# Random-feature attention and a bilinear MLP: norms from bfloat16 halves, q's and k's norms together, a planner with new times and ranks

## The chip, the cores and the metric

One core of a Trainium2 chip runs the whole kernel. The metric is the device time of one execution in microseconds; three executions of the kernel before took 843.41, 843.78 and 844.28 us.

## What is computed

```python
def phi(x):
    proj = np.einsum('bhsd,md->bhsm', x, omega)
    h = proj - np.sum(x * x, axis=-1, keepdims=True) / 2.0
    h = h - np.max(h, axis=-1, keepdims=True)
    return np.exp(h) / np.sqrt(m)
q_p, k_p = phi(q * scale), phi(k * scale)
kv = np.einsum('bhsm,bhsd->bhmd', k_p, v)
z = np.sum(k_p, axis=2)
num = np.einsum('bhsm,bhmd->bhsd', q_p, kv)
den = np.einsum('bhsm,bhm->bhs', q_p, z)[..., None] + 1e-06
x = (num / den).transpose(0, 2, 1, 3).reshape(B * S, H * D)
out = (((x @ w1) * (x @ w2)) @ w3) @ w_out
```

B = 8 batches, H = 8 heads, S = 576 rows, D = 64, m = 128 features; 4608 tokens in all, w1 and w2 are 512x1024, w3 is 1024x1024, w_out is 1024x512. The activations arrive in float32, the weights in float64.

## The kernel before

The 4608 tokens are 36 chunks of 128; a batch is 4.5 chunks. For a chunk of k the kernel projects it on omega (`kpj`), subtracts the maximum (`nm`, L494), adds and takes the exponential (L514, L518) and has the features `ek`; for a batch it sums features times v (`kvp`, L663). A chunk of q goes the same way (`qpj`, `eq`), is turned by two DMA transpositions from SP (`eqT`, L725), and is multiplied with its batch's sums (`nu`, L746). The quotient `xs` is split (`xhl`), turned (`xT`, L804) and enters the gates (`ab`, L981), 256 tokens at a time after the first four chunks. The gates' product goes to `o` (L1022) with the matrix W = w3 w_out, which the kernel forms at the start (`wp`, L932) from weights that it converts from float64 (L828 on ACT, L834 to L854 on DVE).

Precision: where a product is in float16, each operand is two halves, a high part (ACT, or a cast on DVE: L386, L388) and a low part (the difference, on DVE or POOL: L528), and three products are summed. Before a chunk of q or k can be split (`split_raw`, L445: high part L449 on ACT, low part L452 on DVE), it needs a scale, a power of two. `scale` (L430) squares and sums the chunk on ACT into `sums`, `power_of_two` (L348) adds over the partitions by one float32 matmul with ones (L352), and three small steps on DVE (L362 to L366) make the scale of it, a fourth (L440) the factor of the exponential. The first chunks (k below 9, q below 3) are projected in float32 without a scale.

The order of all work is made by `Plan`, in Python, when the kernel is built. Each piece is an operation with an engine (or a choice of engines), a duration in us written beside it, what it reads and writes, and a rank. `order` goes through time: at each moment, each idle engine takes the ready operation of lowest rank whose buffers are free. `LAT` is what passes from an engine's end to the next engine's start, `LANDING` and `US_PER_MB` stand for DMAs. The result is one fixed list per engine, and on the chip each engine works its list off in order. Ranks come from the tables `KRANK`, `QRANK` and `WRANK` for the first chunks and weights, and from `BASE + PERIOD * c` less a lead for the rest. `WEIGHTS_ON_SP` weight blocks are loaded through SP's queue, the others through ACT's; a load has the rank of its block less `FETCH`. `kraw`, `qraw` and `hl` (the split chunks, shared by q and k) have two buffers each, and converted weights pass through three raw buffers.

Of the kernel before, what the change touches and what calls it, by code (L numbers as in the profile page):

```python
# [51 lines left out]
class Plan:  # L52
# [47 lines left out]
    def order(self):  # L100
# [32 lines left out]
        while len(done) < len(self.ops):  # L133
# [5 lines left out]
            for e in ENGINES:  # L139
                if idle[e] > t or not ready[e]:  # L140
                    continue
                for o in ready[e]:
                    took = place(o)
                    if took is not None:
                        break
                else:
# [75 lines left out]
IN_TURN = dict.fromkeys(("kraw", "qraw", "ek", "vraw", "vhl", "kv", "eq", "eqT", "xs", "xhl", "xT", "raw", "mag"), False)  # L222
IN_TURN.update(hl=True, e=True, raw=True, mag=True)


@with_exitstack
def tile_favor_attention_then_bilinear_ffn(
# [65 lines left out]
    def in_pool(pool, shape, dt=F32):  # L293
# [10 lines left out]
        "hl": in_pool(at, (P, 2, NP, P), F16),  # L304
# [43 lines left out]
    def power_of_two(name, cols, keys, n, pre=1.0, add=False, tag="s", n_out=None):  # L348
# [112 lines left out]
    def products(name, c, exact, new=()):  # L461
# [36 lines left out]
    def features(name, c, e, exact, keyed, new=()):  # L498
        pa, pj, nm, factor, key = products(name, c, exact, [e, *new])
        if keyed:  # L500
# [105 lines left out]
    def kv_add(n):  # L606
# [82 lines left out]
    def q_chunk_exact(c):  # L689
# [29 lines left out]
    def q_chunk(c, fast):  # L719
# [3 lines left out]
        for x in range(2):  # L723
# [4 lines left out]
                r=[(t, x)], w=[(u, x)], new=[u] * (x == 0), lat=1.9)  # L728
        eqs[c] = u

    def q_attend(c):
# [68 lines left out]
        if fresh:  # L800
# [165 lines left out]
    def gate(c0, n, u, rank):  # L966
# [4 lines left out]
        for m in range(2):  # L971
            bank = Buf("pm", f"ab_{c0}_{u}_{m}")
            for k in range(nf):
# [92 lines left out]
    om_parts()  # L1066
    for c in range(NCH):
# [5 lines left out]
        else:  # L1073
# [24 lines left out]
    for c in range(NCH):  # L1098
        plan.rank = q_rank(c)
        if c < max(PROJECT_Q, EXACT_Q):  # L1100
            plan.rank -= 20
            load("q", c)
            plan.rank += 20
        else:
# [62 lines left out]
```

## Time and profile before

| | us |
|---|---|
| median of three runs | 843.78 |
| the profiled execution, its own time | 844.44 |
| its span, first to last instruction | 842.3 |
| PE busy | 796.7 (95%) |
| DVE busy | 613.1 (73%) |
| ACT busy | 400.3 (48%) |
| POOL busy | 281.3 (33%) |
| DMA moved | 87.90 MB, mean 104 GB/s |

PE is the matmul engine, PEld its weight loads, which run beside matmuls; SPq and ACTq are the queues from which these engines issue DMAs. A group's busy time counts overlapping instructions once. The granted clock is PE's, as a share of 2.4 GHz; the mean over the run is 0.98. The rows themselves stand below, after the change.

### The profile page before, as it was taken

To read this page: it belongs to the slowest core of one execution; us is meant where nothing else is said; L and a number is where in the kernel's file an instruction comes from. 1 tells how busy PE (TensorE), PEld (TensorE's weight loads), DVE (VectorE), ACT (ScalarE), POOL (GpSimd) and SP (SyncE) were. 2 spreads that over 40 slices of the span, in tenths; PEclk is the share of its full clock that TensorE was granted. 3 is DMA by queue.
4 is the path that set the end of the run, shared out by engine and by line. 5 is a ranking of instruction groups with operands and counts; after the bars stand their busy time and mean duration, and the time that the engine had idled before them with its cause. 6 is when DMAs were issued, how large, how long until landed. Compare 5 with 4: busy or idle time off the path is not lost.

```text
span 842.3 us, 20399 instructions
## 1 busy us (share of the span) xinstructions
PE 796.7 (95%) x8528; PEld 597.6 (71%) x8528; DVE 613.1 (73%) x1177; ACT 400.3 (48%) x697; POOL 281.3 (33%) x287
## 2 busy tenths in 40 slices
PE   3798998899999999999999999899999999999998
PEld 3555546777778777777768677777777777777684
DVE  4889897999969868886769686878696687555200
ACT  3567775665536435543435443745464444322110
POOL 1000001245345253443444453534343533323220
PEclk9598899999999999999999999999999999999999
DMA  9766665114435343534354443433453423322301
GB/s 285 278 234 205 183 181 126 41 41 99 103 62 126 80 98 86 130 90 85 79 82 108 89 76 89 127 77 75 101 127 76 85 61 81 77 52 51 64 26 38
DMA packets 144892, 87.90 MB, mean 104 GB/s; under 512 B 119712, under 2 KB 119840, under 8 KB 144800
## 3 DMA queue, kind: packets, MB, share of 16 engines
q1 hardware_dynamic: 139968, 71.92, 36.5%
q10 hardware_dynamic: 4832, 14.68, 5.1%
q8 instruction: 67, 1.10, 0.6%
q14 instruction: 25, 0.20, 0.1%
HBM read 49.35 MB, written 9.44 MB: 70 GB/s over the span
## 4 chain that ended last, share of the span: by engine, by line
PE 60%; DVE 18%; DMA 10%; issue 5%; POOL 3%; ACT 2%; SPq 1%; ACTq 0%; DVEq 0%; POOLq 0%
PE ab L981 26%; PE o L1022 19%; DMA eqT<-eq 6%; PE wp L932 4%; PE nu L746 3%; DVE nm_q L494 2%; PE kvp L663 2%; PE qpj L481 2%; POOL eq L528 2%; DVE e_q L514 2%; DVE eq L388 2%; DVE vhl L598 1%; DVE w12b L854 1%; PE kpj L481 1%; DVE arena L840 1%
## 5 line engine op out<-in xcount | busy, mean ns | idle before, releaser
L981 PE MATMUL ab<-xT,w12b 128*128 128x256 f16 (+1 forms) x3840 | 397.1, 263 | 5.1 <-ACT asb L993 3.2
L981 PEld LDWEIGHTS <-w12b 128*128 128x128 f16 x3840 | 343.5, 99 | 47.8 <-issue 5.0
L1022 PE MATMUL o<-Wb,arena 128*128 128x512 f16 x864 | 197.1, 379 | 0.6 <-DVE asb L995 0.5
L1001 POOL TENSOR_SCALAR arena<-asb 128x512 f16<-128x512 f32 x72 | 56.2, 781 | 352.2 <-DVE asb L995 280.6
L1022 PEld LDWEIGHTS <-arena 128*128 128x128 f16 x864 | 82.5, 98 | 90.8 <-issue 0.3
L995 DVE TENSOR_TENSOR asb<-ab,asb 128x512 f32<-128x512 f32 x72 | 49.5, 688 | 90.4 <-PE ab L981 83.6
L528 POOL TENSOR_TENSOR ek<-e_k,ek 128x1024 f16<-128x1024 f32 x27 | 59.9, 2220 | 98.0 <-ACT ek L386 56.2
L528 POOL TENSOR_TENSOR eq<-e_q,eq 128x1024 f16<-128x1024 f32 x28 | 66.8, 2384 | 69.5 <-DVE eq L388 55.8
L1003 POOL TENSOR_TENSOR arena<-asb,arena 128x512 f16<-128x512 f32 x72 | 86.8, 1205 | 5.9
L993 ACT ACTIVATE asb<-ab 128x512 f32<-128x512 f32 x72 | 42.8, 595 | 75.5 <-PE ab L981 67.6
L1031 ACT ACTIVATE o<-o,oscs 128x512 f32<-128x512 f32 x36 | 24.7, 685 | 111.0 <-PE o L1022 106.9
L932 PE MATMUL wp<-w12b 128*128 128x512 f32 x128 | 61.6, 631 | 3.7 <-DVE w12b L854 3.7
L518 ACT ACTIVATE e_q<-e_q,ln_e,es_q 128x1024 f32<-128x1024 f32 x31 | 38.3, 1235 | 43.1 <-DVE e_q L514 42.8
L494 DVE TENSOR_REDUCE nm_k<-kpj 128x8 f32<-128x1024 f32 x36 | 43.8, 1216 | 17.9 <-PE kpj L481 14.9
L494 DVE TENSOR_REDUCE nm_q<-qpj 128x8 f32<-128x1024 f32 x36 | 43.9, 1218 | 12.8 <-PE qpj L481 12.2
L932 PEld LDWEIGHTS wp<-w12b 128*128 128x128 f32 x128 | 25.8, 204 | 35.8 <-issue 30.5
L746 PE MATMUL nu<-kv,eqT 128*128 128x65 f16 (+1 forms) x936 | 34.4, 194 | 11.9 <-DMA eqT<-eq 11.9
L746 PEld LDWEIGHTS <-eqT 128*128 128x128 f16 (+1 forms) x936 | 31.3, 100 | 16.8 <-DMA eqT<-eq 13.7
L452 DVE SCALAR_TENSOR_TENSOR hl_q<-qraw,s_q,hl_q 128x512 f16<-128x512 f32 x33 | 41.2, 1247 | 1.4 <-ACT hl_q L449 1.4
L784 ACT ACTIVATE xhl<-xs,p2r_x 128x512 f16<-128x512 f32 x36 | 25.9, 718 | 27.8 <-DVE p2r_x L379 27.3
L518 ACT ACTIVATE e_k<-e_k,ln_e,es_k 128x1024 f32<-128x1024 f32 x27 | 33.3, 1233 | 10.0 <-DVE e_k L514 9.9
L514 DVE TENSOR_TENSOR e_q<-qpj,nm_q 128x1024 f32<-128x1024 f32 x31 | 37.6, 1212 | 0.1
(153 smaller groups left out, 1006.1 us busy)
## 6 DMA issues: line engine op xcount, KB each, us to landing
qraw<-qT SPq DMA_DIRECT2D x36, 256.0 KB, 2.9
kraw<-kT SPq DMA_DIRECT2D x36, 256.0 KB, 2.7
vraw<-v SPq DMA_DIRECT2D x36, 256.0 KB, 3.2
out<-o SPq DMA_DIRECT2D x36, 256.0 KB, 2.1
arena<-w ACTq DMA_DIRECT2D x8, 1024.0 KB, 6.7
arena<-w3T SPq DMA_DIRECT2D x4, 1024.0 KB, 5.2
arena<-w3T ACTq DMA_DIRECT2D x4, 1024.0 KB, 5.7
arena<-wo SPq DMA_DIRECT2D x2, 1024.0 KB, 7.9
```

The costliest lines, as they stand in the source:

```text
L494: one(DVE, 1.22, lambda: nc.vector.tensor_reduce(nm.ap, pj(), AX.X, ALU.max, negate=True), r=[pa], w=[nm], new=[nm])
L514: lambda: nc.vector.tensor_tensor(e.ap, pj(), nm.ap.unsqueeze(2).broadcast_to([P, H, M]), ALU.add),
L518: one(ACT, 1.2, lambda: nc.scalar.activation(e.ap, e.ap, AF.Exp, scale=factor(), bias=ln_e), r=key, w=[e])
L528: (nc.vector if g == DVE else nc.gpsimd).tensor_tensor(f16(t.ap)[:, 1], e.ap, f16(t.ap)[:, 0], ALU.subtract)
L746: nc.tensor.matmul(n_[r0:r1, h // 4, h % 4], f16(t.ap)[:, x, place(h), r0:r1], kv_view(kvs[b])[:, y, h], start=n == 0, stop=n == 2,)
L932: nc.tensor.matmul(bank.ap, w[:, j, k * P : (k + 1) * P], guest[:, j], start=j == j0, stop=j == HALF - 1)
L981: nc.tensor.matmul(dst, w12[m][i][cc][:, a, r * P : (r + 1) * P], x.ap[:, b, cc, off : off + T], start=j == 0, stop=j == len(mm) - 1,)
L993: one(ACT, 0.58, lambda: nc.scalar.mul(asb.ap, ab[0].ap, 2.0**-37), r=[(ab[0], k) for k in ks], w=[asb], new=[asb], rank=first)
L995: one(DVE, 0.69, lambda: nc.vector.tensor_tensor(asb.ap, ab[1].ap, asb.ap, ALU.mult), r=[(ab[1], k) for k in ks], w=[asb], rank=first)
L1001: one(POOL, 0.69, lambda: nc.gpsimd.tensor_scalar(hv()[:, 0], asb.ap, 1.0, 1.0, ALU.mult, ALU.mult), r=[asb], w=[(h, 0)], new=[h], rank=first)
L1003: one(POOL, 1.19, lambda: nc.gpsimd.tensor_tensor(hv()[:, 1], asb.ap, hv()[:, 0], ALU.subtract), r=[asb, (h, 0)], w=[(h, 1)], rank=first)
L1022: nc.tensor.matmul(bank.ap, hs[c, f][1]()[:, a], W[f][:, b], start=f0 + i == 0, stop=f0 + 4 == NF and i == len(mm) - 1,)
```

## The change

A norm's matmul reads only the upper 16 bits of each float32 sum, as bfloat16, and has bfloat16 ones as weights. From k's chunk 9 on, the sums of k's chunk c and of q's chunk c - 5 stand side by side in one `sums` tile, and one norm serves both; q's chunks 3 and 31 to 35 have one of their own. q's and k's split chunks get one buffer each (`hlk`, `hlq`). The planner's latencies, its price of a megabyte, of a transposition (1.9 to 3.2 after 1.3 of issue) and of many operations are others; it knows a backlog of DMAs at which the issuing queue stands, and a slower PE before 36 us. All rank tables, leads and the period are others, the gates of the first four chunks get a rank higher by 8.7, and 10 weight blocks are loaded through SP in place of 6.

```diff
-    LAT = {PE: 0.2, ACT: 0.2, DVE: 0.12, POOL: 0.15, SP: 0.0}
+    LAT = {PE: 0.25, ACT: 0.25, DVE: 0.15, POOL: 0.3, SP: 0.0}
     LANDING = 2.2
-    US_PER_MB = 2.9
+    US_PER_MB = 3.4
+    BACKLOG = 6.0
+    SLOW_PE, SLOW_UNTIL = 1.7, 36.0
...
+                if e == PE and t < self.SLOW_UNTIL:
+                    us *= self.SLOW_PE
                 idle[e] = end = t + us
                 if o.mb:
                     dma = max(end, dma) + o.mb * self.US_PER_MB
+                    idle[e] = max(end, dma - self.BACKLOG)
...
-WEIGHTS_ON_SP = 6
-FETCH = 16.1
+WEIGHTS_ON_SP = 10
+TURNED = 3.2
+FETCH = 22.4
 V_NORM = 7.4
+V_LOAD = 10.0
+FIRST_GATES = -8.7
+AHEAD = 5
...
-QRANK = [-10.8, 48.3, 62.7, 82.0, 108.7, 137.8]
+QRANK = [-6.7, 42.8, 62.7, 86.2, 105.4, 128.4]
...
-PERIOD = 18.4
-LEAD_Q = 67.7
-LEAD_K = 141.9
+PERIOD = 18.0
+LEAD_Q = 79.6
+LEAD_K = 142.8
...
-    "kraw": 2, "qraw": 2, "hl": 2, "e": 2, ...
+    "kraw": 2, "qraw": 2, "hlk": 1, "hlq": 1, "e": 2, ...
...
+    def top_halves(t):
+        return t.bitcast(BF16).rearrange("p (n t) -> p n t", t=2)[:, :, 1]
...
-        one(PE, 0.2, lambda: nc.tensor.matmul(bank.ap[:, 0:n], ones, cols(), start=True, stop=True),
+        one(PE, 0.12, lambda: nc.tensor.matmul(bank.ap[:, 0:n], ones_bf, top_halves(cols()), start=True, stop=True),
...
-        one(DVE, 0.75,
+        one(DVE, 0.75 if c < 9 else 1.35,
...
-            one(ACT, 2.7, exps, r=[pa, nm] + key, w=[e])
+            one(ACT, 2.15, exps, r=[pa, nm] + key, w=[e])
...
-                r=[(t, x)], w=[(u, x)], new=[u] * (x == 0), lat=1.9)
+                r=[(t, x)], w=[(u, x)], new=[u] * (x == 0), lat=TURNED)
...
-            scale([("k", c)])
+            if c - AHEAD < alone:
+                scale([("k", c)])
+            else:
+                q = c - AHEAD
+                plan.rank = q_rank(q) - 25
+                load("q", q)
+                plan.rank = min(q_rank(q), k_rank(c)) - 3
+                scale([("q", q), ("k", c)])
+                plan.rank = k_rank(c) - 3
...
-            gate(c0, n, u, base(c0) + u)
+            gate(c0, n, u, base(c0) + u - FIRST_GATES * (c0 < 4))
```

The lines of the changed kernel are shifted: the norm's matmul L352 is L367 there, the projections L481 are L496, nu L746 is L761, the gates L981 are L996, and the conversion L834, L836, L840, L854 is L849, L851, L855, L869.

**PE, from the projection of q's chunk 10 (`qpj_40`) to its product with the sums (`nu_42`).** Before:

```order
L481 MATMUL qpj_40_3809<-om,hl_q_14_3667 128x128
L352 MATMUL norm_k_78_3838<-sums_k_16_3297,ones 128x1
L352 MATMUL norm_q_79_3841<-sums_q_17_3381,ones 128x1
L981 MATMUL ab_0_0_80_3846<-xT_5_3553,w12b 128x256
L981 MATMUL ab_0_1_81_3880<-xT_5_3553,w12b 128x256
L481 MATMUL kpj_41_3922<-om,hl_k_15_3877 128x128
L981 MATMUL ab_1_0_82_3953<-xT_5_3553,w12b 128x256
L981 MATMUL ab_1_1_83_3989<-xT_5_3553,w12b 128x256
L746 MATMUL nu_42_4020<-kv_4_3569,eqT_11_3951 128x65
```

Now:

```order
L496 MATMUL qpj_40_3630<-om,hlq_q_8_3312 128x128
L996 MATMUL ab_2_1_69_3679<-xT_4_2844,w12b 128x256
L996 MATMUL ab_3_0_70_3716<-xT_4_2844,w12b 128x256
L996 MATMUL ab_3_1_71_3753<-xT_4_2844,w12b 128x256
L1037 MATMUL o_63_3169<-Wb,arena 128x512
L367 LDWEIGHTS ones
L367 MATMUL norm_q_72_3798<-sums_q_10_3223,ones 128x2
L496 MATMUL kpj_41_3800<-om,hlk_k_7_3578 128x128
L367 MATMUL norm_q_73_3833<-sums_q_11_3535,ones 128x2
L996 MATMUL ab_0_0_74_3839<-xT_5_3520,w12b 128x256
L761 MATMUL nu_42_3857<-kv_4_3489,eqT_11_3751 128x65
```

Of each tile one row stands here. A tile `ab` has 24 matmuls each with a weight load, `kpj` 24, `o_63` 12; in the new order 12 of the tile before `ab_2_1` follow the projection first, and 12 of `ab_0_0` stand ahead of nu. The two norms that stood directly behind the projection are now two that each serve a q and a k, further on, and an output block lies in the gap besides.

**SP, its first issues** (loads of 128x2x1024 and 128x4x512 words are weight blocks of 1 MB, those of q, k and v have 0.25 MB). Before:

```order
L428 DMA qraw_1_99<-qT 128x512
L826 DMA arena<-wo 128x2x1024
L394 DMA o_om_raw_116<-omT 64x128 x2
L428 DMA kraw_1_119<-kT 128x512
L560 DMA vraw_1_97<-v 128x8x64
L428 DMA kraw_2_131<-kT 128x512
L560 DMA vraw_2_103<-v 128x8x64
L826 DMA arena<-w3T 128x4x512
```

Now:

```order
L841 DMA arena<-wo 128x2x1024
L443 DMA qraw_1_108<-qT 128x512
L409 DMA o_om_raw_116<-omT 64x128 x2
L841 DMA arena<-w 128x2x1024
L443 DMA kraw_1_129<-kT 128x512
L575 DMA vraw_1_97<-v 128x8x64
L443 DMA kraw_2_135<-kT 128x512
L575 DMA vraw_2_102<-v 128x8x64
L841 DMA arena<-w3T 128x4x512
```

The weight block `wo` comes first, and the block `w`, which ACT's queue loaded at the very start, stands on SP behind omega (`o_om_raw`). Three more loads of v and q (0.75 MB) follow, and then the second block of wo.

**DVE, the conversions ahead of the first product of weights**, which needs two blocks of wo and one of w3T. Before, from the end of the second and third:

```order
L854 SCALAR_TENSOR_TENSOR w12b<-arena 128x1024 x2
L834 TENSOR_SCALAR arena<-arena 128x1024
L836 TENSOR_SCALAR arena<-arena 128x1024
L494 TENSOR_REDUCE nm_k_4_284<-kpj_6_264 128x8
L840 SCALAR_TENSOR_TENSOR arena<-arena 128x1024
L502 TENSOR_SCALAR nm_k_4_284<-nm_k_4_284 128x8
L854 SCALAR_TENSOR_TENSOR w12b<-arena 128x1024
```

Now, from the end of the third:

```order
L869 SCALAR_TENSOR_TENSOR w12b<-arena 128x1024
L849 TENSOR_SCALAR arena<-arena 128x1024
L851 TENSOR_SCALAR arena<-arena 128x1024
L855 SCALAR_TENSOR_TENSOR arena<-arena 128x1024
L509 TENSOR_REDUCE nm_q_4_283<-qpj_6_258 128x8
L869 SCALAR_TENSOR_TENSOR w12b<-arena 128x1024
L517 TENSOR_SCALAR nm_q_4_283<-nm_q_4_283 128x8
```

The maximum of k's third chunk (`nm_k_4`) stood inside the fourth conversion; now that of q's second chunk stands there, and k's third comes two conversions later.

## Rows read from the trace of the kernel before

**Rows 1.** Stretches: from:to, length, busy us (instructions) by engine, clock, DMA share, GB/s.
```profile
0.00:40.00 40.00, 22.11 (x124) 17.20 (x125) 24.98 (x39) 19.43 (x43) 2.33 (x22) 0.76 0.89 284
40.00:60.00 20.00, 20.00 (x73) 10.06 (x73) 16.08 (x19) 10.50 (x20) 0.00 (x0) 0.97 0.68 237
40.00:200.00 160.00, 149.61 (x1460) 102.39 (x1460) 143.76 (x255) 107.60 (x213) 21.56 (x27) 0.95 0.48 142
200.00:750.00 550.00, 536.24 (x6217) 414.64 (x6216) 418.87 (x829) 257.34 (x419) 234.10 (x216) 1.00 0.41 90
```
**Rows 2.** Waits of PE after 200 us: for whom, us in total, times, longest.
```profile
PE nu L746 <- DMA eqT<-eq: 11.9, 15, 2.1
PE o L1022 <- DVE asb L995: 0.5, 2, 0.3
```
**Rows 3.** Waits of PE before 200 us, the four longest in total.
```profile
PE qpj L474 <- DMA o_om_raw<-omT: 10.4, 1, 10.4
PE kvp L613 <- ACT ek_f L507: 5.8, 3, 3.7
PE wp L932 <- DVE w12b L854: 3.7, 1, 3.7
PE ab L981 <- ACT asb L993: 3.2, 2, 1.8
```
**Rows 4.** Timeline at a pair of norms on PE: start us, us, engine, line.
```profile
288.44 0.38 PE L352 MATMUL norm_k<-sums_k,ones 128*128 128x1 f32 x2
288.68 0.36 PE L352 MATMUL norm_q<-sums_q,ones 128*128 128x1 f32 x2
288.91 5.40 PE L981 MATMUL ab<-xT,w12b 128*128 128x256 f16 x48
```
**Rows 5.** Groups by line: shapes, count | busy us, mean ns | idle before.
```profile
L352 PE MATMUL norm_q<-sums_q,ones 128*128 128x1 f32 x66 | 11.6, 246 | 1.2 <-DVE asb L995 0.4 <-DVE es_q L440 0.4 <-DVE l1m L892 0.3
L352 PE MATMUL norm_k<-sums_k,ones 128*128 128x1 f32 x54 | 8.9, 234 | 0.0
L663 PE MATMUL kvp<-vhl,ek 128*128 128x65 f16 x840 | 26.6, 193 | 0.0
L881 PEld LDWEIGHTS <-ones 128*128 128x128 bf16 x16 | 1.3, 103 | 2.2 <-issue 1.8
```
**Rows 6.** Timeline of q's chunk 10, from an output block and its projection to nu.
```profile
284.97 2.76 PE L1022 MATMUL o<-Wb,arena 128*128 128x512 f16 x12
...
287.67 0.84 PE L481 MATMUL qpj<-om,hl_q 64*128 64x128 f16 x24
...
291.90 1.52 DVE L452 SCALAR_TENSOR_TENSOR hl_k<-kraw,s_k,hl_k 128x512 f16<-128x512 f32 x1
...
294.31 2.13 POOL L528 TENSOR_TENSOR eq<-e_q,eq 128x1024 f16<-128x1024 f32 x1 [1.45 <-DVE eq L388]
...
297.39 1.24 SPq L725 DMA_TRANSPOSE eqT<-eq  x1
...
300.27 0.23 PE L746 MATMUL nu<-kv,eqT 128*128 128x65 f16 x2
...
301.00 0.85 PE L746 MATMUL nu<-kv,eqT 128*128 128x65 f16 x22 [0.51 <-DMA eqT<-eq]
```
**Rows 7.** q's turned features (tile eqT): a transposition from issue to landing.
```profile
DMA to landing us min/median/max: 3.0/3.2/5.1
```
**Rows 8.** Timeline of the start: omega's product, DVE's stall, the first product of weights.
```profile
10.39 2.15 PE L474 MATMUL qpj<-o_om_raw,qraw 64*128 64x128 f32 x16 [10.39 <-DMA o_om_raw<-omT]
...
31.58 1.23 DVE L494 TENSOR_REDUCE nm_k<-kpj 128x8 f32<-128x1024 f32 x1 [2.88 <-PE kpj L474]
32.07 1.14 ACT L828 ACTIVATE arena<-arena 128x1024 f32<-128x1024 f32 x1 [2.52 <-DMA arena<-w3T]
...
35.24 2.07 PE L932 MATMUL wp<-w12b 128*128 128x512 f32 x2 [3.72 <-DVE w12b L854]
```
**Rows 9.** Groups by line: the four steps of a conversion on DVE.
```profile
L840 DVE SCALAR_TENSOR_TENSOR arena<-arena 128x1024 uint32<-128x1024 uint32 x20 | 25.0, 1253 | 0.2
...
L854 DVE SCALAR_TENSOR_TENSOR w12b<-arena 128x1024 uint32<-128x1024 uint32 x20 | 24.2, 1220 | 2.5 <-PE wp L932 2.3
...
L836 DVE TENSOR_SCALAR arena<-arena 128x1024 uint32<-128x1024 uint32 x20 | 13.7, 688 | 0.2
L834 DVE TENSOR_SCALAR arena<-arena 128x1024 f32<-128x1024 f32 x20 | 13.7, 687 | 14.6 <-ACT arena L828 14.4
```
**Rows 10.** Waits of 200 to 750 us, one of ACT: us in total, times, longest.
```profile
ACT junk L346 <- DMA kraw<-kT: 31.2, 13, 6.8
```

More of the change, by code (lines that the diff above doesn't have):

```diff
@@ L216 @@
 SLOTS = {
[1 row of a table removed]
+    "kraw": 2, "qraw": 2, "hlk": 1, "hlq": 1, "e": 2, "ek": 6, "vraw": 5, "vhl": 5, "kv": 3, "eq": 1, "eqT": 2,
     "xs": 1, "xhl": 1, "xT": 3, "o": 2, "asb": 2, "pa": 2, "pm": 4,
@@ L221 @@
 }
-IN_TURN = dict.fromkeys(("kraw", "qraw", "ek", "vraw", "vhl", "kv", "eq", "eqT", "xs", "xhl", "xT", "raw", "mag"), False)
-IN_TURN.update(hl=True, e=True, raw=True, mag=True)
+IN_TURN = dict.fromkeys(("kraw", "qraw", "hlk", "hlq", "ek", "vraw", "vhl", "kv", "eq", "eqT", "xs", "xhl", "xT", "raw", "mag"), False)
+IN_TURN.update(raw=True, mag=True)
 @with_exitstack
@@ L303, in tile_favor_attention_then_bilinear_ffn @@
         "qraw": in_pool(at, (P, NP, P)),
-        "hl": in_pool(at, (P, 2, NP, P), F16),
+        "hlk": in_pool(at, (P, 2, NP, P), F16),
+        "hlq": in_pool(at, (P, 2, NP, P), F16),
         "e": in_pool(at, (P, H, M)),
@@ L322, in tile_favor_attention_then_bilinear_ffn @@
     }
-    for name, n in (("sums", 3), ("s", 3), ("es", 3), ("nm", H), ("gd", H), ("gr", H), ("vam", 8)):
+    for name, n in (("s", 2), ("es", 2), ("nm", H), ("gd", H), ("gr", H)):
+        make[name] = in_pool(sm, (P, n))
+    for name, n in (("sums", 2), ("vam", 8)):
         make[name] = in_pool(sm, (P, n))
@@ L486, in products @@
         if exact:
-            one(PE, 1.4, project, r=[raws[name, c], (om_raw, 0), (om_raw, 1)], w=[pa], new=[pa, *new])
+            one(PE, 1.2, project, r=[raws[name, c], (om_raw, 0), (om_raw, 1)], w=[pa], new=[pa, *new])
             factor, key = (lambda: SCALE), []
@@ L522, in in_parts @@
         his = [(DVE, 0.72), (ACT, 1.08)]
-        los = [(DVE, 1.25)] if fast else [(DVE, 1.35), (POOL, 2.13)]
+        los = [(DVE, 1.25)] if fast else [(DVE, 1.35), (POOL, 2.25)]
         op([(g, us, lambda g=g: copy(g, f16(t.ap)[:, 0], e.ap)) for g, us in his],
@@ L616, in add @@
                 )
-        one(PE, 2.2, add, r=[ekf[c], (vraw[c], 0), (vraw[c], 1)], w=[kv_sum], new=[kv_sum] * (n == 0))
+        one(PE, 1.95, add, r=[ekf[c], (vraw[c], 0), (vraw[c], 1)], w=[kv_sum], new=[kv_sum] * (n == 0))
     def kv_exact():
@@ L708, in less @@
                 )
-        one(PE, 1.5, turned, r=[raw, (om_raw, 0), (om_raw, 1)], w=[pt], new=[pt])
-        one(PE, 1.8, less, r=[nm], w=[pt])
+        one(PE, 1.0, turned, r=[raw, (om_raw, 0), (om_raw, 1)], w=[pt], new=[pt])
+        one(PE, 1.2, less, r=[nm], w=[pt])
         one(ACT, 1.15,
@@ L753, in q_attend @@
         if exact:
-            one(PE, 2.2, attend, r=[t, kvf[0]], w=[nu], new=[nu])
+            one(PE, 1.95, attend, r=[t, kvf[0]], w=[nu], new=[nu])
         else:
@@ L807, in q_attend @@
             ),
-            r=[(xhl, 0), (xhl, 1)], w=[(u, c)], new=[u] * fresh, lat=1.9)
+            r=[(xhl, 0), (xhl, 1)], w=[(u, c)], new=[u] * fresh, lat=TURNED)
     w12 = [[[halves(w12b[:, i, n * NC + cc]) for cc in range(NC)] for i in range(2)] for n in range(2)]
@@ L984, in sums @@
                         )
-                one(PE, 0.66 * n, sums,
+                one(PE, 0.645 * n, sums,
                     r=[("b", i, m * NC + cc) for cc in range(NC)] + [(x, c) for c in range(c0, c0 + n)],
@@ L999, in hv @@
             return h.ap.rearrange("p (x i) -> p x i", x=2)
-        one(POOL, 0.69, lambda: nc.gpsimd.tensor_scalar(hv()[:, 0], asb.ap, 1.0, 1.0, ALU.mult, ALU.mult),
+        one(POOL, 0.8, lambda: nc.gpsimd.tensor_scalar(hv()[:, 0], asb.ap, 1.0, 1.0, ALU.mult, ALU.mult),
             r=[asb], w=[(h, 0)], new=[h], rank=first)
@@ L1066, in tile_favor_attention_then_bilinear_ffn @@
     om_parts()
+    alone = max(PROJECT_Q, EXACT_Q, PROJECT_K - AHEAD)
+    for c in range(alone):
+        plan.rank = q_rank(c) - 20
+        load("q", c)
     for c in range(NCH):
@@ L1081, in tile_favor_attention_then_bilinear_ffn @@
         if c not in vraw:
-            plan.rank -= 10
+            plan.rank -= V_LOAD
             v_load(c)
-            plan.rank += 10
+            plan.rank += V_LOAD
         k_chunk(c, c < 9)
@@ L1099, in tile_favor_attention_then_bilinear_ffn @@
         plan.rank = q_rank(c)
[L1100 to L1104, printed above, removed]
+        if c >= max(PROJECT_Q, EXACT_Q):
             plan.rank -= 25
-            load("q", c)
+            if ("q", c) not in raws:
+                load("q", c)
             plan.rank += 22
-            scale([("q", c)])
+            if ("q", c) not in scales:
+                scale([("q", c)])
             plan.rank += 1
```

8 lines of the change are left out of this document (4 added, 4 removed), and 1 row of the table SLOTS.

## The prediction

> **What bounds the kernel now.** Read the stretches first. From 200 to 750 us PE is busy 536.24 of 550 us, at a granted clock of 1.00 (the 2.4 GHz level), while DVE has 418.87 and ACT 257.34 [rows 1]. So there PE's own instructions set the time, and anything that leaves PE's stream shortens the run by as much. Before 40 us PE is busy 22.11 of 40 and its clock averages 0.76, a mix of the 1.2 and the 2.4 GHz level; from 40 to 200 it is busy 149.61 of 160 at 0.95 [rows 1]. The waits of PE say what it stands for. After 200 us it is almost only one thing, q's turned features: 11.9 us in 15 waits of L746 [rows 2]. Before 200 us it is a row of different ones: 10.4 us until omega has landed, 5.8 for the exponentials of k's first chunks, 3.7 for the first product of weights, 3.2 for a free bank of the gates [rows 3]. So three sums: PE's own work, the 15 waits, and the start.
>
> **Norms on PE.** A norm is one float32 product with ones; the trace shows it as two weight loads and two matmuls. Where two stand together, the first begins at 288.44, the second at 288.68, the next gate at 288.91 [rows 4]: 0.235 us each, on a stream that waits for nothing. There are 70 (33 of q, 27 of k, 7 of v, and one each of omega, the first kv and W; rows 5 show 66 matmuls for q's 33 and 54 for k's 27), so 70 x 0.235 = 16.4 us. The change leaves 43: 27 of k are taken with q's, 6 of q, 7, 3. Each becomes one bfloat16 weight load and one matmul of one to eight columns. The trace has no such pair. From below, 840 f16 pairs of 65 columns take 26.6 us, 0.032 us a pair [rows 5]; from above, a bfloat16 load of the same ones takes 0.103 us [rows 5], if nothing hides it. The load of ones is the nearer row, since a matmul of two columns can hide little of the load behind it: I take 0.10, 43 x 0.10 = 4.3 us. Gain 16.4 - 4.3 = 12 us; the ends are 15 (0.032) and, if the bfloat16 form saves nothing at all and only the count falls, 27 x 0.235 = 6.
>
> The Trainium skill, "TensorE: Matmul & The Clock Gate", prices a weight load in two ways: in its section on LDWEIGHTS by columns, 107 ns for 128; in its section on weight-path perf modes at about half of that, when there are 128 weights that are not float32. As an estimate from that page the 43 norms cost 4.6 us by the first and 2.3 by the second, and the sum would be 817 or 815. The trace speaks for the first with the load of ones (103 ns) and for the second with the f16 pairs (32 ns).
>
> **DVE, ACT, POOL.** Sharing a norm drops 27 sets of three small steps and one for the exponent scale. 26 casts go from DVE to ACT, 13 subtractions from POOL to DVE, and 4 weight loads from ACT's queue to SP's. I cost all of this at nothing after 200 us: DVE has 131 us free there, ACT 293 [rows 1]. If that cover went, it would be by order, not by sum; that is the third rival.
>
> **Waits for q's turned features.** Chunk 10 shows the chain. Its projection starts at 287.67, the low half is done on POOL at 294.31 + 2.13 = 296.44, SP issues its transposition at 297.39, and nu, which began at 300.27, goes on at 301.00 [rows 6]: the chain needs 301.00 - 288.51 = 12.5 us from the projection's end (287.67 + 0.84). In that gap PE's order had 96 gate matmuls (48 take 5.40 [rows 4], so 10.8), a projection of k (0.84) and two norms (0.47): 12.1. So nu comes before its data. From issue to landing a transposition takes 3.2 us in the median and up to 5.1 [rows 7], and issuing it costs SP 1.24 [rows 6]; the planner allowed 1.3 and 1.9, and now allows 1.3 and 3.2. It also knows 1.35 us for a split that the trace shows at 1.52 [rows 6], where it had 0.75. The new PE order for chunk 10 has the same 96 gate matmuls, k's projection, two cheap norms and 12 output matmuls (2.76 [rows 6]): 10.8 + 0.84 + 0.2 + 2.76 = 14.6 us, 2 us past the 12.5. Counted so, the gaps of chunks 8 to 35 are mostly 11.5 to 12.1 before, and 13.7 to 20 now. Chunk 10's low half moves to DVE in the new order, after a cast and one more split: about as late as now. I take 10 of the 11.9 us as gained; ends 12 and 4, the latter if the longer gaps only half cover a chain that other steps of DVE lengthen.
>
> **The start.** SP now issues wo before q, and omega after 1.3 MB in place of 2.3 (q, wo, and w from ACT's queue beside them). At 284 GB/s [rows 1] 2.3 MB are 8.1 us, and omega's product began at 10.39 [rows 8], so 2.3 us lie around it; 1.3 MB make 4.6 + 2.3 = 6.9. Then the first product of weights, at 35.24 now [rows 8]. Before it stand four conversions, and DVE idled 2.88 us in the middle of the last, because nm of k's third chunk stood ahead of L840 and that chunk landed late [rows 8]. In the new order that nm stands behind all four. A conversion is 0.687 + 0.688 + 1.253 + 1.220 = 3.85 us of DVE [rows 9]. The last weight block needed, the second wo, has 6.1 MB up to its end on SP: 21.5 + 2.3 = 23.8; ACT's pass 1.14 [rows 8], its own conversion 3.85 and one nm of 1.23 between make 30.0. So PE begins its products about 5 us earlier, and from there its order is dense (before, PE was busy 20.00 of 20 us from 40 to 60 [rows 1]). Not all of this will last: k's fifth chunk is again projected right before the sum that waits for its exponentials, now with two norms between in place of four matmuls. Against that the gates of the first four chunks, pushed back by 8.7 in rank, no longer stand in front of W's last products. I take 5 us; ends 11 (omega's 3.5, the 3.7 for the product and the 3.2 at the gates all gone) and -5, a new wait as long as the 5.8 at the kv sums [rows 3].
>
> **Sum.** The profiled execution took 844.44 us, 0.66 over the median of the runs. 844.4 - 12 - 10 - 5 = 817.4, and against the median 843.8 - 27 = 817 us. Ends: 15 + 12 + 11 = 38 gives 806, 6 + 4 - 5 = 5 gives 839; both at once on all three are unlikely. A change under 0.2% (1.7 us) cannot be told from none here.
>
> **Rivals.**
> First, the order gives nothing: PE stands for as long as before, at other places, since any engine's order is a plan and only PE's work is less. 843.8 - 12 = 832. For it: a transposition lands after 3.0 to 5.1 us [rows 7], and the planner has one number for it. Against it: the waits after 200 us have one cause, and a distance that can be counted.
> Second, the norms are not on the path: nu, or a gate, would end just as late, since the data come when they come. Then the waits grow by what the norms gave up, and 5 + 10 are left: 829. For it: in chunk 10 both norms stand between the projection and the nu that waits, so their going alone would only lengthen that wait. Against: PE has 536 of 550 us of work, and at most 15 of some 40 places have such a wait.
> Third, slower. A norm now waits for two loads and their two sums, and the projection of q follows it closely: at 13 places from 200 us on about 5.3 us of PE's work lie between. The trace's chain from norm (288.44) to split (291.90 + 1.52 = 293.42) is 5.0 us [rows 4, 6]. ACT already stands for k's loads 31.2 us in 13 waits, 2.4 each [rows 10]. If PE stood 2.4 us at 13 places, that is 31 us: 817 + 31 = 848. It decides from 27 / 13 = 2.1 us a place. Against it: k's load is issued 25 ranks ahead of its use, and SP and ACT have room.
>
> **Chances.** Forecast 0.68. First rival 0.14, second 0.09, third 0.07; a start that loses more than the rest gains back to 839 and beyond short of the third, 0.02. Faster by over 0.2%: 0.68 + 0.14 + 0.09 and the little case, less what of them ends within 1.7 us: 0.90. Same: 0.03. Slower: 0.07. The range takes in both middle rivals and leaves out the third, the worst end, and a little beyond the best: 804 to 833.
>
> **What would show it.** Right: PE busy near 785 us; L367 (the norm's new line) with 43 matmuls and next start about 0.1 us behind; waits of L761 (nu) for eqT under 3 us in all; omega's wait near 7 us and the first product of weights near 30. Wrong: waits of L761 for eqT near 10 us again (first rival); a new group of PE waits of L496 for hlq behind DVE (third); norms that stay at 0.2 us each; a first product at 35 us or later; the clock at its lower level for longer between 80 and 160 us.

## Result and profile after

The changed kernel takes 813.75 us in the median of four runs (810.23 to 821.74) beside 843.60 us of the kernel before: a ratio of 0.966, interval 0.958 to 0.974. Nine later runs of the same kernel, in two other sets of runs, gave 814.0 to 821.4; the median of all thirteen is 817.3 us. The forecast was 817. The profiled execution took 816.67 us (span 814.9).

The page of after, its first part (busy us, share of the span, instructions):

```profile
PE 785.3 (96%) x8431; PEld 587.1 (72%) x8431; DVE 591.3 (73%) x1056; ACT 423.6 (52%) x723; POOL 259.3 (32%) x274
```

The stretches of after, columns as in [rows 1]:

```profile
0.00:40.00 40.00, 27.96 (x149) 20.02 (x150) 29.95 (x44) 23.05 (x50) 2.33 (x22) 0.87 1.01 312
40.00:60.00 20.00, 20.00 (x87) 11.25 (x86) 18.15 (x26) 13.59 (x29) 0.00 (x0) 1.00 0.94 287
40.00:200.00 160.00, 150.82 (x1510) 103.89 (x1509) 140.91 (x253) 108.92 (x212) 26.00 (x28) 0.95 0.51 142
200.00:750.00 550.00, 545.28 (x6328) 421.06 (x6327) 412.26 (x745) 283.17 (x449) 218.60 (x210) 1.00 0.39 92
```

In the first 40 us PE works 27.96 us in place of 22.11 and its clock is at 0.87 in place of 0.76; from 200 to 750 it is idle for 4.7 us in place of 13.8 [rows 1].

PE's waits in after, up to 200 us and then all that there are after 200 us:

```profile
PE qpj L489 <- DMA o_om_raw<-omT: 7.0, 1, 7.0
PE kvp L628 <- ACT ek_f L522: 6.1, 3, 3.4
PE nu L761 <- DMA eqT<-eq: 2.7, 2, 1.9
...
PE wp L947 <- DVE w12b L869: 0.3, 1, 0.3
...
PE ab L996 <- DMA xT<-xhl: 2.7, 1, 2.7
PE nu L761 <- DVE kv L696: 1.3, 1, 1.3
PE qpj L496 <- DVE e_k L529: 0.7, 1, 0.7
```

The fifteen waits for q's turned features [rows 2] are gone: none is left after 200 us. Three new ones of 4.7 us together stand there, at other places. Omega is waited for 7.0 us in place of 10.4, the first product of weights 0.3 in place of 3.7 [rows 3].

A place with two shared norms on PE in after (start us, us):

```profile
357.42 2.75 PE L1037 MATMUL o<-Wb,arena 128*128 128x512 f16 x12
360.02 0.17 PE L367 MATMUL norm_q<-sums_q,ones 128*128 128x2 bf16 x1
360.12 0.84 PE L496 MATMUL kpj<-om,hlk_k 64*128 64x128 f16 x24
360.89 0.18 PE L367 MATMUL norm_q<-sums_q,ones 128*128 128x2 bf16 x1
360.93 3.33 PE L996 MATMUL ab<-xT,w12b 128*128 128x256 f16 x29
```

From a norm to the next start on PE 0.10 us pass in front of a projection and 0.04 in front of a gate, where 0.235 passed [rows 4]. The 0.10 is the projection's, not the norm's: from the first of twelve output matmuls to a projection behind them it is 2.70 us here with a norm between, and 2.70 before without one (284.97 to 287.67 [rows 6]). The chain that ended last, by engine, was for 60% on PE before, with 18% on DVE and 10% on DMAs; now:

```profile
PE 84%; DVE 8%; DMA 4%; ACT 2%; issue 1%; SPq 0%; ACTq 0%; DVEq 0%
```

### The profile page after: what moved, and what is told of

Same layout as the page of the kernel before. It is cut to its first block, busy times and chain, and to the rows that moved or that the text cites. A ratio compares the mean times of both kernels' runs of the same rounds, so it can differ in the third digit from the quotient of the medians.

```text
span 814.9 us, 20087 instructions
## 1 busy us (share of the span) xinstructions
PE 785.3 (96%) x8431; PEld 587.1 (72%) x8431; DVE 591.3 (73%) x1056; ACT 423.6 (52%) x723; POOL 259.3 (32%) x274
## 4 chain that ended last, share of the span: by engine, by line
PE 84%; DVE 8%; DMA 4%; ACT 2%; issue 1%; SPq 0%; ACTq 0%; DVEq 0%
PE ab L996 43%; PE o L1037 22%; PE wp L947 5%; PE nu L761 3%; PE qpj L496 3%; PE kvp L678 3%; PE kpj L496 2%; DMA eqT<-eq 2%; DVE arena L855 1%; DVE w12b L869 1%; PE wp L945 1%; ACT ek_f L522 1%; DVE w12b L921 1%; DVE arena L849 1%; DMA arena<-wo 1%
## 5 line engine op out<-in xcount | busy, mean ns | idle before, releaser
L996 PE MATMUL ab<-xT,w12b 128*128 128x256 f16 (+1 forms) x3840 | 395.8, 263 | 6.5 <-DMA xT<-xhl 2.7
L996 PEld LDWEIGHTS <-w12b 128*128 128x128 f16 x3840 | 342.9, 98 | 51.0 <-issue 6.2
L1016 POOL TENSOR_SCALAR arena<-asb 128x512 f16<-128x512 f32 x72 | 60.5, 840 | 379.6 <-DVE asb L1010 234.4
L1018 POOL TENSOR_TENSOR arena<-asb,arena 128x512 f16<-128x512 f32 x72 | 93.6, 1300 | 5.3
L1046 ACT ACTIVATE o<-o,oscs 128x512 f32<-128x512 f32 x36 | 24.7, 686 | 106.7 <-PE o L1037 68.1
L543 POOL TENSOR_TENSOR ek<-e_k,ek 128x1024 f16<-128x1024 f32 x23 | 50.4, 2191 | 88.3 <-ACT ek L401 76.6
L543 POOL TENSOR_TENSOR eq<-e_q,eq 128x1024 f16<-128x1024 f32 x19 | 44.0, 2316 | 54.4 <-DVE eq L403 37.0
L509 DVE TENSOR_REDUCE nm_q<-qpj 128x8 f32<-128x1024 f32 x36 | 43.9, 1218 | 10.3 <-PE qpj L496 10.2
L464 ACT ACTIVATE hlq_q<-qraw,s_q 128x512 f16<-128x512 f32 x33 | 23.7, 719 | 45.6 <-DVE s_q L381 39.5
L779 DVE TENSOR_SCALAR gd<-nu 128x8 f32<-128x8 f32 x36 | 5.9, 165 | 50.7 <-PE nu L761 46.8
L801 DVE SCALAR_TENSOR_TENSOR xhl<-xs,p2r_x,xhl 128x512 f16<-128x512 f32 x36 | 38.1, 1059 | 1.4 <-ACT xhl L799 1.4
L761 PEld LDWEIGHTS <-eqT 128*128 128x128 f16 (+1 forms) x936 | 30.5, 100 | 10.8 <-issue 4.0
L533 ACT ACTIVATE e_k<-e_k,ln_e,es_q 128x1024 f32<-128x1024 f32 x27 | 33.3, 1234 | 7.7 <-DVE e_k L529 7.7
```

Source lines behind the costliest of these rows:

```text
L509: one(DVE, 1.22, lambda: nc.vector.tensor_reduce(nm.ap, pj(), AX.X, ALU.max, negate=True), r=[pa], w=[nm], new=[nm])
L533: one(ACT, 1.2, lambda: nc.scalar.activation(e.ap, e.ap, AF.Exp, scale=factor(), bias=ln_e), r=key, w=[e])
L543: (nc.vector if g == DVE else nc.gpsimd).tensor_tensor(f16(t.ap)[:, 1], e.ap, f16(t.ap)[:, 0], ALU.subtract)
L761: nc.tensor.matmul(n_[r0:r1, h // 4, h % 4], f16(t.ap)[:, x, place(h), r0:r1], kv_view(kvs[b])[:, y, h], start=n == 0, stop=n == 2,)
L996: nc.tensor.matmul(dst, w12[m][i][cc][:, a, r * P : (r + 1) * P], x.ap[:, b, cc, off : off + T], start=j == 0, stop=j == len(mm) - 1,)
L1016: one(POOL, 0.8, lambda: nc.gpsimd.tensor_scalar(hv()[:, 0], asb.ap, 1.0, 1.0, ALU.mult, ALU.mult), r=[asb], w=[(h, 0)], new=[h], rank=first)
```

## Experiments

**Where PE's time went, from the two traces alone.** Give each matmul the distance to the next start that its kind has in an undisturbed stretch at full clock (0.109 us for a gate of 256 columns, 0.216 for an output matmul, 0.43 for a product of weights, and so on), leave the norms out, and subtract the sum up to a time T from T. What is left is PE's lost time up to T: waits, norms and stretches at the lower clock. (The early columns depend on these distances: with others, as reasonable, the kernels differ by 6 us at 60 and 7 at 150; at 200 and 700 the differences stay within 0.5 us.)

| us lost by | 40 | 60 | 150 | 200 | 700 |
|---|---|---|---|---|---|
| before | 21.6 | 20.9 | 32.1 | 33.6 | 68.1 |
| after | 15.5 | 13.8 | 22.8 | 27.2 | 41.0 |
| after, its longest profiled run (821.36 us) | 17.2 | 14.9 | 27.4 | 31.7 | 45.8 |

So 6.4 us come from before 200 us, all of them by 60 us, and 20.7 from 200 to 700. The theory to be tried was the prediction's: norms, waits for turned features and start each give their part, since PE's own work is the bound. Its rivals: norms that are not on the path, and an order that gives nothing or gives by other means than the plan's times.

**1. The norm's form, in the new order.** The changed kernel with float32 norms, still shared:

```diff
-... nc.tensor.matmul(bank.ap[:, 0:n], ones_bf, top_halves(cols()), ...)
+... nc.tensor.matmul(bank.ap[:, 0:n], ones, cols(), ...)
```

> The changed kernel with its norms' matmuls in float32 again (same order, same sharing). Theory, norms lie on PE's path: 43 norms go from about 0.04 us to 0.235 us each, 43 x 0.195 = 8.4 us slower, near 822 us. Rival, norms are covered: no difference, near 814.

Measured: 822.07 us (820.39 to 822.86), 0.974 of before, interval 0.972 to 0.976. That is 8.3 more than the first four runs of the changed kernel and 4.7 more than the median of all thirteen. On the same chip, run 4, which has the changed kernel's norms, took 6.4 us less. PE's busy time rises by 5.4 us (785.3 to 790.7). In this order the form of the norm is on the path.

**2. The norm's form, in the old order.** The kernel before with bfloat16 norms (70, apart), and every engine's order as before:

```diff
-... nc.tensor.matmul(bank.ap[:, 0:n], ones, cols(), ...)
+... nc.tensor.matmul(bank.ap[:, 0:n], ones_bf, top_halves(cols()), ...)
```

> The kernel before with bfloat16 halves in the norms alone (same order on every engine, 70 norms). Theory: PE's stream loses 70 x 0.195 = 13.6 us, and the waits for q's turned features, which come from a chain that starts before the norms, take back 0.3 to 0.5 us at each of 15 places, 5 to 7: near 837 us, waits of nu for eqT 16 to 19 us in all. Rival, norms are off the path: near 844. Rival, nothing is taken back: near 830, waits near 12.

Measured: 842.02 us (839.65 to 844.56) beside 844.28, ratio 0.998, interval 0.997 to 1.000: 2 us. In the traces, what passes from each norm to the next start on PE, waits left out, adds up to 15.1 us before and to 3.6 here, 11.5 less. Its longest waits on PE after 200 us, and its stretch of 200 to 750 us with the columns of [rows 1]:

```profile
PE nu L750 <- DMA eqT<-eq: 12.4, 15, 1.8
PE ab L985 <- DMA xT<-xhl: 1.6, 2, 0.9
```

```profile
200.00:750.00 550.00, 533.40 (x6237) 409.22 (x6235) 420.85 (x837) 258.94 (x421) 235.30 (x218) 1.00 0.41 91
```

PE is idle for 16.6 us in that stretch in place of 13.8 [rows 1]. All its waits, the start's too, add up to 45.8 us in place of 41.6, so they take back about 4 of the 11.5. About 3 more go to the clock: it stands at its 1.2 GHz level for 41 us of the span in place of 34 (mean granted clock 0.976 for 0.980; over all runs of the two kernels 0.976 for 0.979 in the median). The rest, 4 us, is what the profiled execution gained (840.79 for 844.44). Chunk 10 shows a wait taking it back (timeline of PE):

```profile
287.12 0.84 PE L485 MATMUL qpj<-om,hl_q 64*128 64x128 f16 x24
287.90 0.18 PE L356 MATMUL norm_k<-sums_k,ones 128*128 128x1 bf16 x1
287.94 0.16 PE L356 MATMUL norm_q<-sums_q,ones 128*128 128x1 bf16 x1
288.97 5.40 PE L985 MATMUL ab<-xT,w12b 128*128 128x256 f16 x48 [0.87 <-DMA xT<-xhl]
...
300.94 0.85 PE L750 MATMUL nu<-kv,eqT 128*128 128x65 f16 x22 [0.38 <-DMA eqT<-eq]
```

The norms are cheap there (next start 0.04 us behind), the next gate then waits 0.87 us for `xT`, and nu goes on at 300.94, where it did at 301.00 [rows 6]. The prediction's second rival, which was given 829 us, is right in part in the old order: waits end when the data come, and take back what the norms gave up. That the clock takes a share as well was in no theory. The expectation, which had most of the saving arrive (837 us), fell.

**3. The plan's times, with the old ranks.** The kernel before with all of the planner's new durations and latencies, everything else as before (cut):

```diff
-    LAT = {PE: 0.2, ACT: 0.2, DVE: 0.12, POOL: 0.15, SP: 0.0}
+    LAT = {PE: 0.25, ACT: 0.25, DVE: 0.15, POOL: 0.3, SP: 0.0}
...
-                r=[(t, x)], w=[(u, x)], new=[u] * (x == 0), lat=1.9)
+                r=[(t, x)], w=[(u, x)], new=[u] * (x == 0), lat=TURNED)
```

> The kernel before with the planner's new times alone (latencies, price of a megabyte, backlog, slow PE at the start, transposition, split, exponentials and the other durations), old ranks, old norms. Theory, the times set how far apart projection and nu stand: waits of nu for eqT fall from 11.9 to under 4 us, near 836 us. Rival, the ranks do it: waits stay near 12, near 844 us.

Measured: 844.83 us (843.90 to 846.01), ratio 1.000, interval 0.999 to 1.002. PE's waits in it after 200 us:

```profile
PE ab L987 <- DVE es_k L446: 11.0, 1, 11.0
PE norm_q L358 <- DVE es_k L446: 3.9, 3, 1.3
PE kpj L487 <- DVE xs L774: 1.8, 1, 1.8
...
PE nu L752 <- DMA eqT<-eq: 1.2, 2, 1.0
```

As expected the waits for turned features fall, from 11.9 to 1.2 us, but the 836 us expected did not come. Other waits take their place: a norm holds its bank of PSUM, the memory that matmuls write, until DVE has made the exponent factor `es`, the gates take theirs from the same banks, and one gate stands 11.0 us for it. Times alone move the waits; they take none out.

**4. The new ranks, with the old times of q's chain.**

```diff
-TURNED = 3.2
+TURNED = 1.9
...
-        one(DVE, 0.75 if c < 9 else 1.35,
+        one(DVE, 0.75,
...
-            one(ACT, 2.15, exps, r=[pa, nm] + key, w=[e])
+            one(ACT, 2.7, exps, r=[pa, nm] + key, w=[e])
```

> The changed kernel with three old times of the planner (transposition 1.9, split 0.75, exponentials 2.7), new ranks and new norms. Theory, the times do it: waits of nu for eqT come back to 6 us or more, near 821 us. Rival, the longer lead of q's ranks does it: waits under 4 us, near 814.

Measured: 815.72 us (814.37 to 818.13), 0.967 of before, interval 0.964 to 0.970, the changed kernel's own time. The wait in question stays away although the plan again allows 1.9 us (PE's waits after 200 us):

```profile
PE nu L761 <- DMA eqT<-eq: 0.4, 1, 0.4
```

The rival's time and its few waits came, but not by the distance that it named. In q's chunks 8 to 35, read the gap, from the end of the projection to nu's first matmul, and the chain, from the same end to the landing of the second transposition (worked out from the traces, us):

| | gap: median, shortest | chain: median, shortest |
|---|---|---|
| before | 12.0, 11.8 | 12.5, 11.1 |
| run 3: old ranks, new times | 15.7, 12.8 | 13.7, 11.0 |
| run 4: new ranks, three old times | 13.0, 11.3 | 11.9, 9.4 |
| the changed kernel | 15.2, 13.9 | 12.4, 10.1 |

The times set the gap with either ranks: new ones lengthen it by 3.7 us in the old order, three old ones shorten it by 2.2 in the new. Run 4 has few waits all the same because its chain is shorter too, and has ended when nu begins in most chunks: between kernels with like times, the new order has the chain 0.6 us (old ones) and 1.3 us (new ones) shorter. What in the new order does that was not tried; the lead of q alone (79.6 for 67.7) is not needed at that length, since runs 8 and 9 have 70.4 and 74.5 and no such wait over 0.15 us after 200 us.

**5. The start's settings undone** (the old 25 ranks of weight blocks among them):

```diff
-WEIGHTS_ON_SP = 10
+WEIGHTS_ON_SP = 6
...
-FETCH = 22.4
+FETCH = 16.1
...
-FIRST_GATES = -8.7
+FIRST_GATES = 0.0
```

> The changed kernel with the weights' old ranks, 6 blocks on SP, the old lead of their loads and the first gates' old ranks. Theory, the start was worth about 5 us: near 819 us, first product of weights at 33 us or later, in place of 30. Rival, the start is worth nothing, since PE stands later instead: near 814.

Measured: 826.14 us (825.22 to 828.06), 0.978 of before, interval 0.976 to 0.981: 8.7 more than the changed kernel in the same set of runs (817.48). Waits of PE before 200 us, and the stretch of 150 to 200 us:

```profile
PE qpj L489 <- DMA o_om_raw<-omT: 10.0, 1, 10.0
PE ab L996 <- DVE kap L962: 5.0, 1, 5.0
...
PE kpj L496 <- DVE hlk_k L467: 3.6, 1, 3.6
PE wp L947 <- DVE w12b L869: 2.5, 1, 2.5
```

```profile
150.00:200.00 50.00, 40.88 (x661) 34.94 (x660) 46.21 (x90) 32.28 (x59) 15.24 (x19) 0.84 0.43 80
```

By 60 us PE has lost 19.2 us, 5.4 more than after: omega and the first product (33.46) are late again, as the prediction counted them. The rest comes at 150 to 200 us, where PE works 40.88 of 50 us, and with W's last product at 121.0, earlier than after's 123.2. So undone alone the start's settings cost more than they had brought (8.7 us, expected 5); that they fit the other ranks would explain it, but was not tried.

**6. The push of the first gates alone undone** (one number):

```diff
-FIRST_GATES = -8.7
+FIRST_GATES = 0.0
```

> The changed kernel with FIRST_GATES 0.0 for -8.7 alone, so the gates of the first four chunks have their old rank and stand ahead of W's last products again; the loads keep their new order. The run with all four start settings undone (old W ranks, 6 blocks on SP, FETCH 16.1, no push) took 826.1 us, 9 to 12 more than the changed kernel. Theory 1: the push is a large part of that: 821 to 825 us, with the first norms of W's rows and last product of weights later than 123 us by 3 or more, and W's products or scales waited for by L896 or L1037. Rival: the loads' order does it: omega and the first product of weights as early as in the changed kernel (7 and 30 us) keep the time within 3 us of it, 814 to 819.

Measured: 818.14 us (816.04 to 821.31), 0.969 of before, interval 0.967 to 0.972, within 1 us of the median of the changed kernel's thirteen runs (other chips; ratio 0.969 for 0.967). The rival held: the push alone is worth 2 us at most, so the 8.7 us of run 5 need the other three settings, the blocks' ranks, queue and lead. Those undone with the push kept was not run. What the push moves is a loss in time, 20.6 us lost by 150 and 32.5 by 200, beside 22.8 and 27.2.

**7. Norms apart again.** The changed kernel with 70 bfloat16 norms, and the same with float32 (so only times, ranks, loads and buffers are left of the change):

```diff
-                scale([("q", q), ("k", c)])
+                scale([("q", q)])
+                scale([("k", c)])
```

> The changed kernel with a norm of its own for q and for k (70 bfloat16 norms). Theory, only PE's stream counts: 27 more norms of 0.04 us, 1 us slower, near 815. Rival, a norm also holds a bank and four small steps of DVE, and gates wait for the bank: waits of gates or norms for L455 of 4 us or more, near 819.

> The changed kernel with 70 norms of their own in float32, that is, only the planner's times, ranks and the split buffers of the change. Theory, norms add to PE's stream once the order is without stalls: 813.75 + 70 x 0.235 - 43 x 0.04 = 828.5. Rival, the order carries nearly all (the kernel before gave back most of the norms' saving): near 816.

Measured, in one set of runs: 827.75 us (827.10 to 830.48; ratio 0.981, interval 0.978 to 0.983) and 835.38 us (832.88 to 839.03; 0.989, 0.986 to 0.993), beside 817.48 of the changed kernel, run once more:

> The changed kernel once more, to see how far its runs lie apart (810 to 822 in four) and where: 814 in the median; if the spread is in the start, the wait for xT of 2.7 us after 200 us and the clock between 60 and 160 us differ from the first profile.

The order alone gives 8.5 us (843.93 to 835.38), the form 7.6, sharing 10.3. The last is ten times what 27 norms at 0.04 us weigh on PE. Most of it is one cause in the bfloat16 form, two waits of W's scales (L896) at 134 to 147 us, PE's longest before 200 us; during the first, with PE standing, the clock falls once more (139 to 153 us). The two, added up:

```profile
PE l L896 <- ACT asb_wab L888: 9.5, 2, 6.7
```

**8. Norms apart, with ranks to suit.** Is that sharing itself, or ranks that fit shared norms alone? The kernel of 7 with bfloat16, and seven numbers chosen anew with the planner:

```diff
-V_NORM = 7.4
+V_NORM = 4.1
...
-BASE = 106.6
+BASE = 103.9
...
-LEAD_Q = 79.6
+LEAD_Q = 70.4
...
```

> The changed kernel with the 43 norms taken apart to 70 again (bfloat16, as in the run before with separate norms, which took 827.75 us), but with seven rank numbers chosen anew for this form (V_NORM 4.1, BASE 103.9, LEAD_Q 70.4, two of KRANK, one of QRANK, one more of KRANK). Theory 1: sharing itself is worth only PE's time for 27 norms, 27 x 0.035 = 1 us; the other 10 us of the run with separate norms were an order that no longer fitted (9.5 us of waits of the W scales' products L896 for ACT's L888). Then this kernel comes back to 816 to 821 us, and the waits of L896 for asb_wab fall below 3 us. Rival: the separate norms cost engines other than PE (27 more norms wait for a bank and for three more DVE steps each), whatever the ranks: then it stays at 825 to 829, with waits of L367 or L996 for L455 (es) of several us after 200 us.

Measured: 821.16 us (820.03 to 825.55; ratio 0.972, interval 0.970 to 0.975) beside 817.63 of the changed kernel on the same chip, run a third time:

> The changed kernel unaltered, beside the two others on one chip: 813 to 818 us by both theories.

PE's waits in the kernel with new ranks, before 200 us and, the last row, after:

```profile
PE ab L996 <- DVE l1m L907: 4.6, 2, 2.5
...
PE l L896 <- ACT asb_wab L888: 1.7, 1, 1.7
...
PE norm_k L367 <- DVE es_q L455: 2.8, 1, 2.8
```

Ranks alone bring back 6.6 of the 10.3 us, and the wait for L888 is 1.7 us. It lands at the upper edge of the first theory. What is left for sharing is about 3.5 us: by the trace 1 of PE's stream and one wait of 2.8 us for a bank, which the rival names. That these two make it up was not tried.

**9. Ranks nudged.** Three waits of 4.7 us are left after 200 us, so a little was to be had (two of k's ranks besides, 137.8 and 141.5 to 141.0 and 138.7):

```diff
-V_LOAD = 10.0
+V_LOAD = 10.2
...
-PERIOD = 18.0
-LEAD_Q = 79.6
-LEAD_K = 142.8
+PERIOD = 18.13
+LEAD_Q = 74.5
+LEAD_K = 141.6
```

> The changed kernel with PERIOD 18.13 for 18.0, LEAD_Q 74.5 for 79.6, LEAD_K 141.6 for 142.8, V_LOAD 10.2 for 10.0 and two of k's ranks moved (138.7 and 141.0 for 141.5 and 137.8). Theory 1 (PE is at its floor after 200 us, 5 us of stalls in 610): within 3 us of the changed kernel, 812 to 819. Rival: q's shorter lead by 5 brings waits of nu (L761) for eqT back, 3 us or more of them after 200 us, and the time rises past 820.

Measured: 812.02 us (810.76 to 814.54), 0.961 of before, interval 0.959 to 0.964; beside 817.63 (814.04 to 821.36) of the changed kernel on that chip it is 5.6 us less. PE's only wait after 200 us, and the stretch behind it:

```profile
PE qpj L496 <- DVE xs L783: 0.2, 1, 0.2
```

```profile
200.00:300.00 100.00, 100.00 (x1172) 77.47 (x1165) 79.21 (x146) 53.09 (x85) 45.93 (x42) 1.00 0.47 104
```

No wait for turned features after 200 us came back with a lead shorter by 5, so there was room in it. The gain is more than the 3 us that the first theory allowed; most of it is those waits, which are 4.5 us in the changed kernel's profile on that chip. This version beats both kernels; what it has left to gain lies before 200 us, where PE has lost 27.4 us.

## Why the prediction was right, step by step

| step | forecast, us | measured, us |
|---|---|---|
| norms | 12 (6 to 15) | 13 |
| waits after 200 us | 10 (4 to 12) | 9 |
| start | 5 (-5 to 11) | 4 |

**Norms: right, with two errors that cancel.** From each norm to the next start on PE, waits left out, the traces add up to 15.1 us for the 70 norms before and to 3.1 for the 43 now: 12.0 us, where I had 16.4 - 4.3. I read 0.235 us at a pair behind a projection [rows 4] and took it for all. Eleven pairs stand between two gates and take 0.366 us, 0.183 a norm:

```profile
275.17 0.28 PE L352 MATMUL norm_k<-sums_k,ones 128*128 128x1 f32 x2
275.31 0.36 PE L352 MATMUL norm_q<-sums_q,ones 128*128 128x1 f32 x2
275.53 1.14 PE L981 MATMUL ab<-xT,w12b 128*128 128x256 f16 x9
```

The new norm was priced too high: 25 of the 43 have the next start 0.025 to 0.041 us behind, 12 have it at 0.10, the six others at 0.12 to 0.22. For the 25 the f16 pairs of [rows 5] were the nearer row. The 12 all stand in front of a projection, which reads 64 partitions, and there the norm costs next to nothing: without one, a projection starts 0.312 us behind an output matmul, where another output matmul or a gate starts 0.216 behind it, in both traces; with the norm between it is 0.216 + 0.099 = 0.315. Three norms stood so before and twelve do now, so counting that (nine times 0.096), the gain is 13 us. The Trainium skill, "TensorE: Matmul & The Clock Gate", makes such a load 107 ns by its section on LDWEIGHTS and about half in that on weight-path perf modes. The 25 norms lie below both; the 12 lie near the first, but by the projection behind them.

That the norms' gain arrives depends on the order, and the step did not say so: it held PE's 536 busy us of 550 to be enough. Run 2 shows that it is not. In the old order the new form freed 11.5 us and brought 2 (4 in the profiled execution); waits took back 4, the clock 3, a term that the prediction did not have. In the new order it freed 7.3 us and brought 5 to 8 (run 1), with norms apart 10.5 and 7.6 (run 7). The second rival was right in part for the kernel before and wrong where the order had its waits out.

**Waits after 200 us: right, with a part left out.** From 200 to 750 us PE is idle for 4.7 us in place of 13.8, 9 less: 11.9 us of waits for eqT are gone, three others of 4.7 have come. The prediction laid the longer gaps to the times in the plan, and the traces bear that out with either ranks (run 4). It named the price of the transposition (1.9, now 3.2) first; runs 3 and 4 change others with it, so its own share is not shown. What the step left out is that times alone move the waits (run 3), and that the new order has the chain shorter as well, at like times (table of run 4). The first rival, an order that gives nothing, falls with run 7: with norms as before the order gives 8.5 us, though with ranks that were made for shared ones.

**The start: right.** Omega's product began at 7.03 (forecast 6.9) and the first product of weights at 30.14 (30.0; the profiles of the two later sets have 28.9 and 31.6, so that this one met the forecast to 0.1 us is chance):

```profile
7.03 2.15 PE L489 MATMUL qpj<-o_om_raw,qraw 64*128 64x128 f32 x16 [7.03 <-DMA o_om_raw<-omT]
...
30.14 2.07 PE L947 MATMUL wp<-w12b 128*128 128x512 f32 x2 [0.31 <-DVE w12b L869]
```

PE has 6 to 7 us less lost by 60 us. By 200 us 6.4 are left, and 2.2 of them are norms (11 with 2.8 us to the next start, now 8 with 0.6): 4 us for the start. "Not all of this will last" came true, but not at the place it was put to: PE waits 2.7 us for eqT before 200 us, while the kv sums wait 6.1 us in place of 5.8. The push of the first gates, which the prediction counted in favour, gives 2 us at most (run 6). The sign against it, a lower clock from 80 to 160 us, did not come (mean 0.95, before 0.92).

**The rival on the other side** did not come: no row of after has L496 waiting for `hlq`. The bfloat16 form with norms apart has one such wait of 1.1 us, where the rival had thirteen of 2.4.

So 13 + 9 + 4 = 26 of the 27.8 us between the two profiled executions (844.44 - 816.67); the rest lies in distances too short to tell from the matmuls' own. That the forecast of 817 meets the median of thirteen runs, 817.3, is closer than its steps came to theirs and than the runs, 810 to 822 us, lie to each other: that part is chance.

## What to carry to other kernels

An instruction that leaves the busiest engine shortens the run by its full time only where that engine's order has no waits for data behind it (here 2 to 4 of 11.5 us with such waits, 5 to 8 of 7.3 without); take out the waits first, or both together, and measure a saving in the order in which it is to stay. Durations in a planner and ranks are one setting: new times with old ranks gave nothing here, and three old times with the new ranks gave all. Price an instruction by what the stream takes with it and without it, not by the distance behind it alone. After a change to what the plan contains, choose the ranks anew before judging the change.

## What the runs showed of the chip

- A bfloat16 matmul of 128x128 ones on two columns is recorded with 0.17 us and its load with 0.098, but has the next start only 0.03 to 0.04 us behind it.
- A projection on 64 partitions starts about 0.096 us later than a matmul on 128 would, in the cases here: 0.312 us for 0.216 behind an output matmul and 0.205 for 0.109 behind a gate; behind a norm that follows an output matmul it is 0.099 for 0.028.
- Thirteen runs of one kernel spread over 810 to 822 us, and the granted clock goes with them: 0.985 in the two runs of 810, 0.977 in those of 821. The longest profiled one lost its time before 200 us (table above). Two stretches of 10 us in it, and then the same two in the changed kernel's first profile:

```profile
20.00:30.00 10.00, 7.51 (x41) 7.17 (x42) 8.75 (x12) 7.24 (x20) 0.00 (x0) 0.59 1.06 377
100.00:110.00 10.00, 6.40 (x32) 3.48 (x33) 6.14 (x14) 2.32 (x4) 0.00 (x0) 0.83 0.85 258
```

```profile
20.00:30.00 10.00, 7.70 (x48) 7.13 (x48) 8.78 (x10) 6.64 (x20) 0.00 (x0) 0.70 1.06 380
100.00:110.00 10.00, 10.00 (x24) 4.43 (x24) 9.47 (x18) 4.21 (x8) 0.00 (x0) 1.00 0.65 172
```

The clock is at its lower level for more of the first stretch, PE's products of weights come 1.5 us later (31.6 for 30.1), and at 100 us PE stands for 3.7 us for q's turned features (0.9 in the first profile); the clock falls again behind that stand, at 103.8. Why they came late, and what set the longer first spell, is open.
- A transposition of q's features lands after 2.7 to 7.9 us in after, in the median 2.9:

```profile
DMA to landing us min/median/max: 2.7/2.9/7.9
```

The plan has one number for it.
